# A linear-attention and SwiGLU kernel on one core: one more unit by squares, two more k turned through DRAM, and another set of weight pieces with signs by ScalarE

## The chip, the core and the metric

The kernel runs on one NeuronCore of a Trainium2 chip. The metric is the device time of one execution in microseconds (us). TensorE (PE) multiplies matrices and transposes by multiplying with an identity, VectorE (DVE) and ScalarE (ACT) work elementwise, GpSimd (POOL) and SyncE (SP) mainly issue DMAs. Each engine takes its instructions in the order in which they stand in its own queue and waits for semaphores of the others. A difference of less than some 0.2% can't be told from no change here.

## The reference

For 4 batches, 8 heads, 768 positions and head size 48 the reference runs a gated recurrence. Its output, 3072 tokens of 384 features, goes through a SwiGLU block with 1536 hidden features.

```
f = 1.0 / (1.0 + np.exp(-f_logit))
for t in range(S):
    state = f[:, :, t, :, None] * state + np.einsum('bhd,bhe->bhde', k[:, :, t], v[:, :, t])
    y[:, :, t] = np.einsum('bhd,bhde->bhe', q[:, :, t], state)
x = y.transpose(0, 2, 1, 3).reshape(B * S, H * D)
out = (silu(x @ w_gate) * (x @ w_val)) @ w_out
```

q, k, v and f_logit are float32. The three weight matrices come as float64, 8 bytes an element, and the kernel turns them into float32 itself.

## The kernel before

**Units.** The sequence is cut into 6 chunks of 128 positions. A unit is one batch's chunk, numbered u = 4 c + b for chunk c and batch b: units 0 to 3 are the first chunk, 4 to 7 the second, 8 to 11 the third. `attention(u)` (L576) is a generator of 15 steps that the caller spreads over time. In order: Sigmoid of f; gate turned into head-by-time form; k turned; reverse scan of the gates (`tail`); kT; (turn of kT); forward scan; q turned; qT and the decayed state; scores `sc` on TensorE; mask A; outputs y; the state's product dS; the new state.

**Two ways to turn f, k and q.** Time runs along the partitions when they are loaded, and the products want the features there. A plain unit loads them as they are, and TensorE transposes them: `fTp` (L614), `kTp` and `qTp` (L657, L658), four 128x128 transposes each. A unit by squares (`by_squares`, L403) loads them with four neighbouring positions side by side (L446 to L455), so that VectorE can transpose blocks of 32x32 (L630, L641, L685). Before, units from 5 on go by squares.

**Two ways to turn the decayed k back.** dS needs kT with time on the partitions again. Either TensorE transposes it (`kt`, L704) and ScalarE copies it out (L717), or the unit is `turned` (L634): VectorE transposes 32x32 blocks into `beside`, in the room of the raw k (L668), four DMAs write them to DRAM (L671), and one more reads them back as `kt` (L709 or L715). Before, units 5, 6, 7 and 10 to 19 are turned. In the second chunk the queue for that is GpSimd's, later SyncE's.

**Weights.** 18 pieces (`weight_piece`, L459): two column blocks each of w_gate and w_val in turn (pieces 0 to 11), then w_out (12 to 17). A piece is fetched by SyncE into one of four buffers. `sizes` (L487) on ScalarE makes the low bits (`up`) and the absolute value (`top`); `join` (L498) on VectorE clamps `top`, shifts it and adds `up`. The signs come either from VectorE (L514, one more instruction there, and the shift also masks, L512) or, for the pieces in `SIGNED` (L532), from ScalarE (L494) ahead of `top`; the shift is then L508. Pieces 0 and 1 are handled in two halves.

**Order of the work.** First the four units of chunk 0 (L1270 to L1294), with the first loads on SyncE's and GpSimd's queues (`load_ahead`, L1261) and the first sizes and joins. Then `mlp_plain` (L830) runs the block's 24 gate and val products for chunk 0 and its 12 down steps. For the other chunks, `mlp_fifteen` (L1006) computes each product of 3x3 by 3x2 blocks with 15 multiplications instead of 18, and `down_seven` (L1128) those of 2x2 blocks with seven instead of eight; both need sums of weight blocks, made by VectorE (`weight_sums`, L966). Everything else is put between TensorE's steps by hand-written times: in `in_turn_of_time` (L1222) each TensorE step has a nominal length, and whatever has a time at or below the sum so far is written into the queues ahead of the next step. `EARLY` (L937) holds the times of units 4 to 7, `SIZES_AT`, `JOINS_AT`, `FETCHES_AT` (L934 to L936) those of the weight pieces, `SUMS_AT` those of the weight sums, `CHAINS` (L913) those of the later units. An entry is only a place in the order; on the chip an instruction runs when its queue and its inputs let it. The order is held fast on TensorE, VectorE, ScalarE and SyncE (L1308, L1347); GpSimd's is free in the first stage apart from the chained loads (L454).

Of the kernel before, what the change touches and what calls it, by code (L numbers as in the profile page):

```python
# [13 lines left out]
AF = mybir.ActivationFunctionType  # L14
# [276 lines left out]
def short_path(ctx, tc, ident, least, judge, q, k, v, f_logit, moe_w_gate, moe_w_val, moe_w_out, out):  # L291
# [9 lines left out]
    nc = tc.nc  # L301
    B, H, S, D = q.shape
    C = 128
    NCH = S // C
# [7 lines left out]
    N1 = C + 1  # L312
    NRAW = 2
    NROT = 2
    NV = 4
    SQUARES = 2
# [23 lines left out]
    raw = {nm: [both_raw[nm][:, i] for i in range(NRAW)] for nm in "qkf"}  # L340
# [23 lines left out]
    def pairs(t, off=0):  # L364
        return t[:, off:off + HP * N1].rearrange("p (a t) -> p a t", t=N1)
# [35 lines left out]
    rooms = {nm: t.rearrange("p n h w -> p (n h w)")[:, 0:Q + HP * RUN] for nm, t in both_raw.items()}  # L401

    def by_squares(u):  # L403
        return u >= SQUARES * B - 3

    def make_rooms(pool):
        for nm in "fkq":
# [25 lines left out]
    def load(u, what="fkqv"):  # L433
        b, c = units[u]
        rows = slice(c * C, (c + 1) * C)
        inputs = dict(f=f_logit, k=k, q=q, v=v)
        for nm in "fqkv" if c >= SQUARES else "fvkq" if by_squares(u) else "fkqv":
            src = inputs[nm]
            if nm not in what:
                continue  # L440
            if nm == "v":
                dst = v_of(u)
            elif not by_squares(u):
                dst = raw[nm][u % NRAW]
            else:
                since = len(traced)  # L446
                for n in range(4):
                    at = Q * (1 - n % 2)
                    (nc.sync if c >= SQUARES else nc.gpsimd).dma_start(
                        out=rooms[nm][Q * n:Q * (n + 1), at:at + HP * RUN].rearrange("t (a e) -> t a e", a=HP),  # L450
                        in_=src[b, n // 2::2, rows, :].rearrange("a (t i) d -> t a (i d)", i=NI))
                if c < SQUARES:
                    by_pool.extend(ins for ins in traced[since:] if ins.engine == mybir.EngineType.Pool)
                    keep_order(by_pool[-5:])  # L454
                continue  # L455
            queue = nc.gpsimd if nm == "v" and c < SQUARES and (by_squares(u) or u in (1, 2)) else nc.sync
            queue.dma_start(out=dst[:, :, 0:D], in_=src[b, :, rows, :].rearrange("h t d -> t h d"))

    def weight_piece(dst, src, parts, signs):  # L459
# [69 lines left out]
    NW = 2  # L529
    FIRST = 2  # L530
    NPART = 2
    SIGNED = (4, 6, 7, 8, 9, 11, 15, 16, 17)  # L532

    def add_piece(dst, src, parts=1):
        fetch, *rest = weight_piece(dst, src, parts, len(fetches) in SIGNED)
        fetches.append(fetch)
        for group, fs in zip((sizes, joins), rest):
            group += fs
# [19 lines left out]

    def bank(name):
        return banks[-1].tile([128, 512], FP32, tag="a", name=name)  # L560

    ahead = set()

    def sigmoid_ahead(u):


        fr = raw["f"][u % NRAW]
        nc.scalar.activation(fr, fr, AF.Sigmoid)
        ahead.add(u)

    owner = {}

# [3 lines left out]
    def attention(u):  # L576
        b, c = units[u]
        rot = u % NROT if c < SQUARES else 0
        fr, kr, qr = (raw[nm][u % NRAW] for nm in "fkq")
        v_ = v_of(u)  # L580
        gate, tail = (x[u % NROT if c < SQUARES else 0] for x in (gates, tails))
# [3 lines left out]
        in_squares = by_squares(u)  # L585
# [32 lines left out]
        if in_squares:  # L618
            nc.scalar.activation(squares("f"), squares("f"), AF.Sigmoid)
            if c >= SQUARES and b == (c > SQUARES):  # L620

                nc.scalar.activation(spare, spare, AF.Silu)
        else:
            p = transposed("fTp", fr)
            for part in parts:
                nc.scalar.activation(pairs(gate)[:, part, 1:N1], p[:, part], AF.Copy if u in ahead else AF.Sigmoid)
        yield
        owner["gate", rot] = u
        if in_squares:
# [1 line left out]
            load_after(u, "f")  # L631
        yield

        turned = SQUARES * B + 2 <= u < (NCH - 1) * B or c < SQUARES and in_squares  # L634
        turn_queue = nc.sync if c >= SQUARES else nc.gpsimd
        kT = att.tile([128, HP, C], FP32, tag="kT", name="kT")
        qT = att.tile([128, HP, C], FP32, tag="qT", name="qT", bufs=2)
# [63 lines left out]
        if c < NCH - 1 and not turned:  # L701
            p = bank("kt")
# [27 lines left out]
        if c and b < B - 1:  # L730
# [20 lines left out]
            for h in range(H):  # L751
                a, par = h // 2, h % 2
                f = h * D
# [30 lines left out]
        if c < NCH - 1:  # L784
            p = bank("dS")
# [117 lines left out]
    def chain(k, q, qmul, turn=None, head=None):  # L903
        return (*[k + t for t in STEPS], turn or k + 3.5, head or k + 3.5, q, qmul)
# [6 lines left out]
        ((PRODUCT - 0.05, "b"), (between[1], "o"), (between[3], "o"), (down[3], "A")),  # L911
        *[((down[10] - whole, "A"), (between[1], "o"), (between[3], "o"), (down[3], "A"))] * (NCH - 4)))}
    CHAINS = {c: chains for c, chains in zip(range(2, NCH), (  # L913
        (chain(2.6, 4, 8.6), chain(14.5, 20, 23), chain(30, 37, 43.2), chain(57.4, 57.8, 61)),
        (chain(-12, -8.5, -5), chain(3.5, 6, 9), chain(16, 28, 33, 21.5, 23.5), chain(40.1, 53, 55, 44.5, 52)),
        *[(chain(-19.4, -11.2, -9.5), (-7.5, -6.3, 1.3, 2.2, 3.2, 5.5, 8, 10), chain(16, 28, 33, 21.5, 23.5), chain(40.1, 53, 55, 44.5, 52))] * (NCH - 4)))}
    LAST = 72.5
# [9 lines left out]
    def score_bank(u):  # L927
# [3 lines left out]
            return bank("sc")  # L931
        return {"o": banks_o, "A": banks_a}[kind].tile([128, 512], FP32, tag=kind, name="sc")

    JOINS_AT = (0.8, 4.5, 5, 7.6, 13.2, 16.3, 20.3, 27.2, 29.6, 36.1, 38.7, 43.3, 46.6, 47.8, 55.3, 55.4, 67.6, 70.8)  # L934
    SIZES_AT = (0.39, 2.4, 6.2, 11.1, 13.2, 18.4, 18.6, 22.1, 31.8, 38, 39.8, 40.1, 43.1, 50.8, 53, 56, 64.8)
    FETCHES_AT = (-1.1, 0.6, 5.5, 5.9, 6, 9.2, 10.6, 21.1, 23.6, 27, 35.5, 35.5, 37.8, 42.4)  # L936
    EARLY = (  # L937
        (-1.01, 4.17, 4.58, 9.7, 9.87, 10.5, 11, 11.5, 12, 13.4, 17.3, 22, 28.4, 28.41, 33),
        (26, 31.3, 32.8, 34.3, 34.6, 34.6, 36.1, 37.4, 38.2, 40.6, 43.3, 43.4, 50.8, 54.81, 56),
        (46.2, 49.2, 50.7, 51.4, 51.5, 57, 57.6, 58, 62, 63.9, 64.4, 65.5, 68.2, 68.21, 70),  # L940
        (63, 64, 66.8, 66.9, 67.4, 67.9, 68.6, 71.6, 73.3, 75.9, 76, 76.7, 78, 78.41, 80.3))
    SUMS_AT = (64.3, 64.5, 72.58, 72.7, 74.06, 74.74, 75.3, 75.42, 75.98, 76.02, 76.18, 76.3, 76.66, 76.86,
        77.34, 77.54, 78.22, 78.5, 79.18, 79.86, 81.22, 81.26, 81.26, 81.34, 81.62, 81.9, 81.94, 82.58, 82.58, 82.7,
        83.2)
    LATE_SUMS_AT = (23,)
    FINISH = (3, 5, 6, 7, 9, 10)
    DOWN_SUMS_AT = (5.2, 5.21, 18.8, 18.81, 34.5, 34.51, 43, 43.01)
    sums = {}

    def plus(dst, a, b):  # L950
# [310 lines left out]
    def load_ahead(u):  # L1261

        if u + NRAW < B:
            load(u + NRAW, "fkq")
        load(u + 1, "v")
        fetches.pop(0)()
        if u + NRAW == B:
            load(u + NRAW, "fkq")

    run(0, 0, 1, 2)  # L1270
    load_ahead(0)
# [11 lines left out]
            sizes.pop(0)()  # L1283
        run(b - 1, 4)
    first_join = joins.pop(0)
    first_join(("clamp"))
    sizes.pop(0)()
    run(B - 1, 3)
    first_join(("add"))
    joins.pop(0)()  # L1290
    next(first[B - 1])
    sizes.pop(0)()
# [2 lines left out]

    waiting = [(t, sizes.pop(0)) for t in SIZES_AT]
    waiting += [(t, joins.pop(0)) for t in JOINS_AT]
    waiting += [(t, fetches.pop(0)) for t in FETCHES_AT]
    assert not fetches and not sizes and not joins
    waiting.append((-0.02, lambda: sigmoid_ahead(B)))  # L1300
    for b, at in enumerate(EARLY):
        run_of = attention(B + b)
        waiting += [(t, lambda run_of=run_of: next(run_of)) for t in at]
# [1 line left out]
    sums = sums_of[0][0:7] + sums_of[1][0:7] + sums_of[0][7:] + sums_of[1][7:]  # L1305
    waiting += zip(SUMS_AT, sums[:len(SUMS_AT)])
    in_turn_of_time(waiting, mlp_plain(0))
# [17 lines left out]
    waiting = []  # L1325
# [4 lines left out]

    assert len(SUMS_AT) + len(LATE_SUMS_AT) == len(sums)
    waiting += zip(LATE_SUMS_AT, sums[len(SUMS_AT):])
    waiting += [(at, f) for at, f in zip(DOWN_SUMS_AT, down_weight_sums())]
    blocks = {}
# [90 lines left out]
```

## Time and profile before

| what | us |
|---|---|
| median of 3 runs | 597.67 (597.44 to 597.67) |
| the profiled execution | 597.51 |
| its span, first to last instruction | 595.8 |
| TensorE busy | 585.5 |
| VectorE busy | 479.3 |
| ScalarE busy | 301.1 |
| GpSimd busy | 112.8 |
| first gate product starts | 29.62 |
| first product of the fifteen starts | 138.44 |

The profiled execution's own time is its span and 1.7 us around it. The stages follow one another: the first chunk's units to 29.6 us, the plain block on chunk 0 with units 4 to 7 beside it to 138 us, then one round for each later chunk. Times in the trace count from the span's start. A timeline row gives start, length, engine, line of the kernel, operation, output<-input, shape and count, and in brackets the idle time of the engine just before it with what ended it. A row of a group gives busy time, mean ns of one instruction, and the idle time before. In the list of waits a row gives who waited for whom, the sum in us, how often, and the longest.

### The profile page before, as it was taken

What the parts mean: (1) busy time and instruction counts of PE and PEld (TensorE: products, weight loads), DVE (VectorE), ACT (ScalarE), POOL (GpSimd) and SP (SyncE); (2) the same over time, 40 slices, a digit from 0 to 9 for tenths busy, and PEclk for the clock granted to TensorE, in tenths of its full rate; (3) what the DMA queues carried; (4) which work ended last, traced back from release to release, by engine and by line L of the source; (5) the groups of instructions that cost most, each with busy time, mean ns of one, the idle gap of its engine ahead of it and who ended that gap; (6) DMA issues with size and microseconds to landing.
All of it is one profiled execution on the core that took longest, in us unless ns stands there. A gap on an engine that the chain in (4) does not pass through costs nothing.

```text
span 595.8 us, 10874 instructions
## 1 busy us (share of the span) xinstructions
PE 585.5 (98%) x3972; PEld 481.8 (81%) x3972; DVE 479.3 (80%) x830; ACT 301.1 (51%) x563; POOL 112.8 (19%) x240
## 2 busy tenths in 40 slices
PE   7899999999999999999999999999999999999996
PEld 4744444667888999888999888899988899988896
DVE  7997998999989877998986888994978972666741
ACT  3488677025877322676640667632476730356600
POOL 3140345202132330212030030330030330000000
PEclk9999999999999999999999999999999999999999
DMA  9999487233666565542345332543231100100001
GB/s 205 253 307 286 142 217 186 60 98 107 122 117 110 96 150 136 138 100 64 84 117 137 99 80 62 112 111 99 74 99 28 29 10 6 53 2 1 2 1 56
DMA packets 106291, 61.86 MB, mean 104 GB/s; under 512 B 64200, under 2 KB 97032, under 8 KB 106232
## 3 DMA queue, kind: packets, MB, share of 16 engines
q1 hardware_dynamic: 93800, 45.96, 31.0%
q0 software_dynamic: 10992, 13.19, 10.0%
q10 hardware_dynamic: 1440, 1.97, 0.9%
q8 instruction: 32, 0.52, 0.4%
q14 instruction: 27, 0.22, 0.1%
HBM read 47.64 MB, written 8.13 MB: 94 GB/s over the span
## 4 chain that ended last, share of the span: by engine, by line
PE 98%; DVE 1%; ACT 0%; issue 0%; DVEq 0%
PE o L1151 20%; PE A L1052 18%; PE B L1052 15%; PE c L1052 6%; PE o L1052 6%; PE o L859 5%; PE gate L836 5%; PE val L836 5%; PE sc L700 4%; PE o L1214 3%; PE y L746 3%; PE y L767 2%; PE dS L787 2%; PE y L742 2%; PE kt L704 1%; PE fTp L614 0%
## 5 line engine op out<-in xcount | busy, mean ns | idle before, releaser
L757 POOL DMA_DIRECT2D xT<-yT x120 | 59.8, 506 | 53.4 <-ACT yT L750 49.0
L1052 PE MATMUL A<-xs,w_both 128*128 128x256 f32 x240 | 62.2, 382 | 0.0
L1151 PE MATMUL o<-w_out,h 128*128 128x192 f32 x360 | 62.0, 327 | 0.0
L1151 PEld LDWEIGHTS o<-w_out,h 128*128 128x128 f32 x360 | 58.7, 190 | 1.0 <-issue 0.2
L1057 ACT COPY c<-A 128x512 f32<-128x512 f32 x40 | 23.3, 583 | 60.5 <-PE A L1052 59.4
L1057 ACT COPY aside<-A 128x512 f32<-128x512 f32 x60 | 35.2, 586 | 32.9 <-PE A L1052 32.7
L951 DVE TENSOR_TENSOR c<-c,aside 128x512 f32<-128x512 f32 x60 | 41.1, 685 | 12.8 <-ACT aside L1057 11.1
L1052 PEld LDWEIGHTS A<-xs,w_both 128*128 128x128 f32 x240 | 44.9, 190 | 6.6
L1004 DVE TENSOR_TENSOR h<-h,c 128x256 f32<-128x256 f32 x100 | 40.6, 414 | 7.6 <-ACT h L1068 7.3
L954 DVE TENSOR_TENSOR c<-c,aside 128x512 f32<-128x512 f32 x60 | 41.0, 684 | 2.7 <-ACT aside L1057 2.7
L1068 ACT ACTIVATE h<-c 128x256 f32<-128x256 f32 x100 | 39.4, 417 | 5.0 <-DVE c L951 3.8
L719 DVE TENSOR_TENSOR A<-sc,causal 128x512 f32<-128x512 f32 x48 | 30.9, 685 | 13.4 <-PE sc L700 13.4
L1151 PE MATMUL o<-ws,h 128*128 128x192 f32 x240 | 41.5, 328 | 0.0
L1052 PE MATMUL B<-xs,w_both 128*128 128x256 f32 x160 | 41.3, 380 | 0.0
L1052 PE MATMUL A<-xs,extra 128*128 128x256 f32 x160 | 41.2, 380 | 0.0
L1052 PE MATMUL c<-xT,w_both 128*128 128x256 f32 x160 | 41.1, 379 | 0.0
L1052 PE MATMUL B<-xT,extra 128*128 128x256 f32 x160 | 41.0, 379 | 0.0
L1057 ACT COPY aside<-B 128x512 f32<-128x512 f32 x60 | 35.2, 586 | 9.0 <-PE B L1052 7.0
L1151 PEld LDWEIGHTS o<-ws,h 128*128 128x128 f32 x240 | 39.1, 190 | 0.5
L954 DVE TENSOR_TENSOR c<-o,c 128x512 f32<-128x512 f32 x40 | 27.4, 686 | 11.0 <-ACT h L1068 6.2
L951 DVE TENSOR_TENSOR c<-c,o 128x384 f32<-128x384 f32 x15 | 8.2, 548 | 34.8 <-PE o L1151 34.8
L690 POOL MEMSET gates<- 128x4 f32 x24 | 3.6, 150 | 169.0 <-DVE qT L593 163.9
(163 smaller groups left out, 1240.2 us busy)
## 6 DMA issues: line engine op xcount, KB each, us to landing
fsquares<-in_f_logit_dram SPq DMA_DIRECT2D x64, 96.0 KB, 4.1
qsquares<-in_q_dram SPq DMA_DIRECT2D x64, 96.0 KB, 2.3
ksquares<-in_k_dram SPq DMA_DIRECT2D x64, 96.0 KB, 2.4
w<-in_moe_w_gate_dram SPq DMA_DIRECT2D x6, 768.0 KB
w<-in_moe_w_val_dram SPq DMA_DIRECT2D x6, 768.0 KB, 6.5
w<-in_moe_w_out_dram SPq DMA_DIRECT2D x6, 768.0 KB, 8.8
v<-in_v_dram SPq DMA_DIRECT2D x19, 192.0 KB, 2.8
turn<-ksquares SPq DMA_DIRECT2D x40, 64.0 KB, 2.2
```

The lines of the kernel that those rows point to most:

```text
L700: nc.tensor.matmul(sc[par][:, a * C:(a + 1) * C], lhsT=kT[r, a, :], rhs=qT[r, a, :], start=True, stop=True)
L719: nc.vector.tensor_tensor(A[:, par], sc[par].rearrange("p (a t) -> p a t", t=C), causal.unsqueeze(1).broadcast_to((128, HP, C)), ALU.mult)
L757: (nc.gpsimd if c >= SQUARES else nc.sync).dma_start(out=xT[c][f % 128:f % 128 + n, f // 128, b * C:(b + 1) * C], in_=yT[r:r + n, par, a / ...
L836: nc.tensor.matmul(p, lhsT=w[:, j, i, :], rhs=xT[c][:, i, :], start=(i == 0), stop=(i == KT - 1))
L859: nc.tensor.matmul(p, lhsT=hidden_tile(h, n // 2)[:, n % 2 * 2 + b // 2, b % 2 * C:(b % 2 + 1) * C], rhs=w_out[:, j, :], start=(n == 0), s ...
L951: nc.vector.tensor_tensor(dst, a, b, ALU.add)
L954: nc.vector.tensor_tensor(dst, a, b, ALU.subtract)
L1004: lagging.append(lambda: f(*args))
L1052: nc.tensor.matmul(p[name][:, n, :], lhsT=weights_of[a][:, n, j, :], rhs=tokens[b], start=fresh and n == 0, stop=True, skip_group_check=True)
L1057: nc.scalar.copy(t, p[name])
L1068: nc.scalar.activation(dst, src[:, 0, :], AF.Silu)
L1151: nc.tensor.matmul(p[:, n, :], lhsT=lhsTs[j][:, n * C:(n + 1) * C], rhs=rhs[:, j, :], start=first and j == order[0] and n == 0, stop=j == ...
```

## The change

- `by_squares` holds from unit 4 on, so unit 4's f, k and q are loaded in squares (from inside unit 3's step with kTp and qTp), its kT is turned through DRAM on GpSimd's queue, and its three sets of TensorE transposes and its kt go.
- Units 8 and 9 are turned through DRAM, too, on SyncE's queue.
- v of units 1 and 2 is loaded on SyncE's queue instead of GpSimd's, v of unit 4 on GpSimd's.
- `sigmoid_ahead`, a Sigmoid in place on the raw f of unit 4, is taken out.
- `SIGNED` names twelve pieces (0, 1, 2, 3, 5, 6, 9, 10, 11, 15, 16, 17) instead of nine (4, 6, 7, 8, 9, 11, 15, 16, 17).
- The tables of times change: weights, units 4 to 7, weight sums, and the chains of units 8, 9 and 10.

```diff
--- before.py
+++ after.py
@@ -401,7 +401,7 @@
     rooms = {nm: t.rearrange("p n h w -> p (n h w)")[:, 0:Q + HP * RUN] for nm, t in both_raw.items()}
 
     def by_squares(u):
-        return u >= SQUARES * B - 3
+        return u >= B
 
     def make_rooms(pool):
         for nm in "fkq":
@@ -453,7 +453,7 @@
                     by_pool.extend(ins for ins in traced[since:] if ins.engine == mybir.EngineType.Pool)
                     keep_order(by_pool[-5:])
                 continue
-            queue = nc.gpsimd if nm == "v" and c < SQUARES and (by_squares(u) or u in (1, 2)) else nc.sync
+            queue = nc.gpsimd if nm == "v" and c < SQUARES and by_squares(u) else nc.sync
             queue.dma_start(out=dst[:, :, 0:D], in_=src[b, :, rows, :].rearrange("h t d -> t h d"))
 
     def weight_piece(dst, src, parts, signs):
@@ -529,7 +529,7 @@
     NW = 2
     FIRST = 2
     NPART = 2
-    SIGNED = (4, 6, 7, 8, 9, 11, 15, 16, 17)
+    SIGNED = (0, 1, 2, 3, 5, 6, 9, 10, 11, 15, 16, 17)
 
     def add_piece(dst, src, parts=1):
         fetch, *rest = weight_piece(dst, src, parts, len(fetches) in SIGNED)
@@ -558,15 +558,6 @@
 
     def bank(name):
         return banks[-1].tile([128, 512], FP32, tag="a", name=name)
-
-    ahead = set()
-
-    def sigmoid_ahead(u):
-
-
-        fr = raw["f"][u % NRAW]
-        nc.scalar.activation(fr, fr, AF.Sigmoid)
-        ahead.add(u)
 
     owner = {}
 
@@ -623,7 +614,7 @@
         else:
             p = transposed("fTp", fr)
             for part in parts:
-                nc.scalar.activation(pairs(gate)[:, part, 1:N1], p[:, part], AF.Copy if u in ahead else AF.Sigmoid)
+                nc.scalar.activation(pairs(gate)[:, part, 1:N1], p[:, part], AF.Sigmoid)
         yield
         owner["gate", rot] = u
         if in_squares:
@@ -631,7 +622,7 @@
             load_after(u, "f")
         yield
 
-        turned = SQUARES * B + 2 <= u < (NCH - 1) * B or c < SQUARES and in_squares
+        turned = SQUARES * B <= u < (NCH - 1) * B or c < SQUARES and in_squares
         turn_queue = nc.sync if c >= SQUARES else nc.gpsimd
         kT = att.tile([128, HP, C], FP32, tag="kT", name="kT")
         qT = att.tile([128, HP, C], FP32, tag="qT", name="qT", bufs=2)
@@ -911,7 +902,7 @@
         ((PRODUCT - 0.05, "b"), (between[1], "o"), (between[3], "o"), (down[3], "A")),
         *[((down[10] - whole, "A"), (between[1], "o"), (between[3], "o"), (down[3], "A"))] * (NCH - 4)))}
     CHAINS = {c: chains for c, chains in zip(range(2, NCH), (
-        (chain(2.6, 4, 8.6), chain(14.5, 20, 23), chain(30, 37, 43.2), chain(57.4, 57.8, 61)),
+        (chain(2.6, 4.8, 8.6), chain(14.5, 21.7, 23.2, 21.2, 19.6), chain(29.2, 37, 43.6), chain(57.4, 55.8, 61)),
         (chain(-12, -8.5, -5), chain(3.5, 6, 9), chain(16, 28, 33, 21.5, 23.5), chain(40.1, 53, 55, 44.5, 52)),
         *[(chain(-19.4, -11.2, -9.5), (-7.5, -6.3, 1.3, 2.2, 3.2, 5.5, 8, 10), chain(16, 28, 33, 21.5, 23.5), chain(40.1, 53, 55, 44.5, 52))] * (NCH - 4)))}
     LAST = 72.5
@@ -931,20 +922,20 @@
             return bank("sc")
         return {"o": banks_o, "A": banks_a}[kind].tile([128, 512], FP32, tag=kind, name="sc")
 
-    JOINS_AT = (0.8, 4.5, 5, 7.6, 13.2, 16.3, 20.3, 27.2, 29.6, 36.1, 38.7, 43.3, 46.6, 47.8, 55.3, 55.4, 67.6, 70.8)
-    SIZES_AT = (0.39, 2.4, 6.2, 11.1, 13.2, 18.4, 18.6, 22.1, 31.8, 38, 39.8, 40.1, 43.1, 50.8, 53, 56, 64.8)
-    FETCHES_AT = (-1.1, 0.6, 5.5, 5.9, 6, 9.2, 10.6, 21.1, 23.6, 27, 35.5, 35.5, 37.8, 42.4)
+    JOINS_AT = (0.8, 2.1, 5, 7.6, 11.6, 15.9, 20.3, 25.6, 26, 34.9, 37.9, 42.9, 46.6, 48.2, 55.3, 55.4, 66.8, 70)
+    SIZES_AT = (0.39, 2.4, 6.2, 11.1, 13.2, 18.4, 18.6, 19.1, 30.2, 36.4, 38.2, 38.5, 43.1, 50.8, 54.2, 56, 66.8)
+    FETCHES_AT = (-1.1, 0.6, 5.9, 6.3, 7.2, 8.8, 10, 21.5, 23.6, 25.2, 29.3, 32.7, 40.8, 46.2)
     EARLY = (
-        (-1.01, 4.17, 4.58, 9.7, 9.87, 10.5, 11, 11.5, 12, 13.4, 17.3, 22, 28.4, 28.41, 33),
-        (26, 31.3, 32.8, 34.3, 34.6, 34.6, 36.1, 37.4, 38.2, 40.6, 43.3, 43.4, 50.8, 54.81, 56),
-        (46.2, 49.2, 50.7, 51.4, 51.5, 57, 57.6, 58, 62, 63.9, 64.4, 65.5, 68.2, 68.21, 70),
-        (63, 64, 66.8, 66.9, 67.4, 67.9, 68.6, 71.6, 73.3, 75.9, 76, 76.7, 78, 78.41, 80.3))
-    SUMS_AT = (64.3, 64.5, 72.58, 72.7, 74.06, 74.74, 75.3, 75.42, 75.98, 76.02, 76.18, 76.3, 76.66, 76.86,
-        77.34, 77.54, 78.22, 78.5, 79.18, 79.86, 81.22, 81.26, 81.26, 81.34, 81.62, 81.9, 81.94, 82.58, 82.58, 82.7,
-        83.2)
-    LATE_SUMS_AT = (23,)
+        (-0.02, 1, 3.6, 4.7, 6, 6.01, 7.2, 10.2, 10.2, 13.4, 17.3, 22, 29.6, 29.61, 35),
+        (26.4, 30.1, 31.6, 33.1, 34.2, 34.2, 35.7, 37.4, 37.8, 40.2, 44.1, 44.2, 51.6, 55.21, 58.2),
+        (46.2, 49.2, 51.5, 52.2, 52.3, 55, 55.2, 55.6, 59.6, 63.1, 63.6, 64.7, 67.4, 67.41, 69.2),
+        (62.2, 63.2, 66, 66.1, 66.6, 67, 67.1, 70, 72.5, 75.1, 75.6, 77.61, 78.3, 79.2, 80.3))
+    SUMS_AT = (63.5, 63.7, 71.78, 71.9, 73.26, 73.94, 74.5, 74.62, 75.18, 75.22, 75.38, 78.54, 78.74, 79.3,
+        79.42, 79.46, 79.46, 79.66, 79.7, 80.1, 80.38, 81.06, 82.02, 82.14, 82.42, 82.54, 82.78, 84.78, 85.26,
+        85.4, 86.5)
+    LATE_SUMS_AT = (22.25,)
     FINISH = (3, 5, 6, 7, 9, 10)
-    DOWN_SUMS_AT = (5.2, 5.21, 18.8, 18.81, 34.5, 34.51, 43, 43.01)
+    DOWN_SUMS_AT = (5.2, 5.21, 20.7, 20.71, 34.5, 34.51, 43, 43.01)
     sums = {}
 
     def plus(dst, a, b):
@@ -1262,10 +1253,9 @@
 
         if u + NRAW < B:
             load(u + NRAW, "fkq")
-        load(u + 1, "v")
+        if not by_squares(u + 1):
+            load(u + 1, "v")
         fetches.pop(0)()
-        if u + NRAW == B:
-            load(u + NRAW, "fkq")
 
     run(0, 0, 1, 2)
     load_ahead(0)
@@ -1283,10 +1273,10 @@
             sizes.pop(0)()
         run(b - 1, 4)
     first_join = joins.pop(0)
-    first_join(("clamp"))
+    first_join(("clamp",))
     sizes.pop(0)()
     run(B - 1, 3)
-    first_join(("add"))
+    first_join(("add",))
     joins.pop(0)()
     next(first[B - 1])
     sizes.pop(0)()
@@ -1297,7 +1287,6 @@
     waiting += [(t, joins.pop(0)) for t in JOINS_AT]
     waiting += [(t, fetches.pop(0)) for t in FETCHES_AT]
     assert not fetches and not sizes and not joins
-    waiting.append((-0.02, lambda: sigmoid_ahead(B)))
     for b, at in enumerate(EARLY):
         run_of = attention(B + b)
         waiting += [(t, lambda run_of=run_of: next(run_of)) for t in at]
```

## The prediction, made before the result was known

> **What bounds the kernel now.** I read the busy shares and the chain of waits first, then TensorE's waits, then each engine in order of time over 0 to 240 us.
>
> ```profile
> span 595.8 us, 10874 instructions
> PE 585.5 (98%) x3972; PEld 481.8 (81%) x3972; DVE 479.3 (80%) x830; ACT 301.1 (51%) x563; POOL 112.8 (19%) x240
> PE 98%; DVE 1%; ACT 0%; issue 0%; DVEq 0%
> PE idle L362 <- DVE floor L354: 2.1, 1, 2.1
> PE sc L700 <- DVE qT L593: 1.6, 2, 0.8
> PE fTp L614 <- DMA fraw<-in_f_logit_dram: 0.6, 1, 0.6
> ```
>
> The chain that ends last is 98% TensorE, and its few waits all lie before 29 us. The answer that adds busy time by stretch gives TensorE 30.00 of 30.00 us in each stretch from 30 us on, up to 500. So from the first gate product (29.62) to the last product (591) the time is the sum of what TensorE is given. An edit gains only if it takes instructions off TensorE, or, before 29.6 us, shortens the chain that leads there. It loses if an instruction that TensorE waits for comes after its place in TensorE's order. Busy time of a matmul overlaps that of the next, so I price TensorE work by the distance of starts:
>
> ```profile
> 39.92 0.60 PE L614 MATMUL kTp<-idf,kraw 128*128 128x128 f32 x4
> 40.36 0.60 PE L614 MATMUL qTp<-idf,qraw 128*128 128x128 f32 x4
> 40.80 5.32 PE L836 MATMUL gate<-xT,w_both 128*128 128x512 f32 x12
> 46.04 1.16 PE L700 MATMUL sc<-qT,kT 48*128 48x128 f32 x16
> 47.13 0.66 PE L704 MATMUL kt<-idf,kT 128*128 128x128 f32 x4
> 47.62 5.32 PE L836 MATMUL val<-xT,w_both 128*128 128x512 f32 x12
> ```
>
> Four transposes cost 0.44 us (39.92 to 40.36) or 0.49 us (47.13 to 47.62), though each is listed with 273 ns.
>
> **What the Trainium skill says.** "TensorE: Matmul & The Clock Gate", section Part 4: PE-mode transpose, puts one transpose at about 275 ns inside a kernel; the trace agrees on the duration (272 to 273 ns), but four in a row advance TensorE by only 440 to 490 ns, which is what I use. "VectorE: DVE Perf Modes", section The three transpose paths: VectorE transposes only within 32x32 blocks, hence the second half of the turn by DRAM; the trace shows it at 0.69 to 1.11 us for 128x512. "DMA: Bandwidth & Descriptors", section Issuing engines are not separate DMA queues: all queues end in the same 16 engines, so another queue saves issue time only. The trace agrees: the DMA share is 0.91 to 1.10 in every stretch from 15 to 60 us, whoever issues. "ScalarE: Activation LUTs", section Table sets, says that cheap functions lie in every set. The trace has a Sign at 66.12 between the Sigmoid of 60.04 and the next table load at 68.03, so signs ahead of the first Silu need no load.
>
> **The change, part by part.**
>
> 1. *Transposes off TensorE.* Unit 4 (first of the second chunk) loses fTp (29.13 to 29.62, 0.49), kTp and qTp (39.92 to 40.80, 0.88) and kt (47.13 to 47.62, 0.49). Units 8 and 9 lose kt (151.72 to 152.21 and 169.82 to 170.31, 0.49 each). Sum: 0.49 + 0.88 + 3 x 0.49 = **2.84 us**, all on the path.
>
> 2. *What fTp(4) covered.* It stood between dS(3) and the first gate product, which also needs ScalarE's copy of xT (28.67 to 29.15). dS(3) hands over at 29.12, so some 0.07 us of that copy comes into view.
>
> 3. *Signs.* The list goes from nine pieces to twelve: 0, 1, 2, 3, 5, 10 join it, 4, 7, 8 leave. Pieces 0 and 1 come in two halves.
>
> ```profile
> L494 ACT ACTIVATE up<-w,middle 128x768 f16<-128x768 uint16 x9 | 10.3, 1144 | 0.0
> L491 ACT ACTIVATE up<-w 128x384 uint16<-128x384 uint32 x4 | 2.6, 645 | 0.0
> L514 DVE TENSOR_SCALAR up<-w 128x768 uint16<-128x768 uint16 x7 | 4.2, 601 | 0.0
> L514 DVE TENSOR_SCALAR up<-w 128x384 uint16<-128x384 uint16 x4 | 2.3, 587 | 0.0
> L630 DVE STREAM_TRANSPOSE gates<-fraw 128x512 f32<-128x512 f32 x3 | 3.3, 1113 | 0.0
> L641 DVE STREAM_TRANSPOSE qT<-kraw 128x512 f32<-128x512 f32 x3 | 2.1, 684 | 0.0
> L685 DVE STREAM_TRANSPOSE tails<-qraw 128x512 f32<-128x512 f32 x3 | 2.1, 693 | 0.0
> L668 DVE STREAM_TRANSPOSE kraw<-kT 128x512 f32<-128x512 f32 x3 | 2.1, 706 | 0.0
> ```
>
> VectorE saves the sign step (0.62 between starts) but the shift then costs 0.59 instead of 0.47, so about 0.5 a piece or half: 4 halves + 4 - 3 = 5, or 2.5 us. ScalarE gains 4 half signs and one whole net. A half sign isn't in the trace; its ends are 0.50 (the half `up` start to start, 22.54 to 23.04) and 0.65 (that row's duration); I take 0.55. So 2.2 + 1.0 = +3.2 us; kt copies of units 4, 8, 9 (0.5 each) and the spare Sigmoid of L568 (0.5) leave, so -2.0.
>
> 4. *Unit 4 on VectorE.* Added: transposes of f 0.96, k 0.60, q 0.70, kT 0.63 and the small copy 0.07, by distance of starts in unit 5 (64.04 to 73.10): about +3.0 us. With part 3, +0.5 us up to 60 us, where VectorE idles 4.5 us at 56.2 to 60.8 for val. The stretch that matters is 28 to 45 us. I laid the new order out by hand from these distances. ScalarE: xT copied 29.05, third half 30.5, Sigmoid(4) 31.2, last half 32.8, piece 2 at 35.6, table load and first Silu 37.2, piece 3 at 40.0. VectorE: half joins and f's transpose to 34.1, k's transpose and scan to 36.0, piece 2 joined 38.1, kT 39.3, kT turned and second scan 41.2, piece 3 joined 43.2, q's transpose 43.9, **qT(4) done 44.6**. TensorE: gate from 29.15, four steps of 2.575, then 5.24 for two, so **sc(4) at 44.7**. Gates 2 and 3 want piece 2 at 39.45 (1.3 us to spare), the vals behind sc(4) want piece 3 at about 45.8 (2.6). sc(4) meets qT(4) almost to the tenth: I book 0.1 us, with ends 0 and 0.8.
>
> 5. *Loads.* f, k, q of unit 4 leave SyncE's queue (19.11 to 25.02) for GpSimd's, in runs of 768 instead of 192 bytes; v(4) goes there too; v(1) and v(2) go to SyncE's. f(4) may start once fTp(3) is through (18.2). The issue takes 2.2 us and the landing 7.3 more (page, fraw by POOL), so it should land near 28 to 30, before Sigmoid(4) wants it at 30.7: nothing booked. k(4) and q(4) follow kTp(3) and qTp(3) (22.7), wanted at 34 and 43. v(2), behind q(3) on SyncE (issued by 16.3), takes 4.0 to 7.0 to land; y(2) wants it at 22.77 and TensorE idles 0.79 after dS(2): nothing booked, ends -0.2 and +1.2. The weight fetches behind them wait on the same full engines as before.
>
> 6. *Before the gate.* Piece 0's sign step stood ahead of mask A(3) on VectorE (26.13 to 26.60), while sc(3) ended at 26.41: -0.1 us. Otherwise VectorE's own chain of about 5.13 us a unit sets this stage.
>
> 7. *Units 8 and 9.* VectorE +0.63 each for kT; TensorE gives 0.49 each. SyncE gets four turn DMAs and a kt load each (2.64 + 0.67), with k(9), k(10) and q behind them; units 10 to 19 already run so without a TensorE wait. qT(9) was done 166.5 for sc(9) at 168.73: 2.2 us less 2 x 0.63 less 0.49 leaves 0.5. VectorE is nearly full from 150 to 168, and TensorE's banks wait for ScalarE's copies, which wait for VectorE to free their buffers, so I book 0.2, ends 0 and 1.2.
>
> 8. *Retimed steps.* y(5) moves one step of TensorE's order later; weight sums move up to 3 us. The odd sums are wanted only at the third triple (138.4 + 26), so nothing is late: 0.
>
> Sum: -2.84 + 0.07 + 0.1 - 0.1 + 0.2 = **-2.57 us**. The profiled execution took 597.51 (span 595.8 and 1.7 around it): 594.94. The median, 597.67, is 0.16 above it: **595.1**.
>
> **Rivals.**
>
> *Partial give-back.* TensorE has less work but waits at sc(4), sc(9) or y(2). For: qT(4) has 0.1 us in hand and VectorE is over 90% busy in these stretches. Against: VectorE idles 4.5 us soon after. Price: the upper ends 0.8 + 1.2 with half of y(2)'s 1.2 give 2.6, less the 0.3 booked, half taken: +1.2, so 596.3.
>
> *f(4) behind others on GpSimd's queue, slower than before.* Sigmoid(4) stands on ScalarE ahead of the last half of val's first piece and of piece 2. If f(4) lands at L, qT(4) comes at 44.6 + (L - 30.7), and sc(4) holds TensorE as long. It eats the whole gain from L = 33.3. That happens if f(4) is issued behind the clearing of gates(3):
>
> ```profile
> 25.65 0.21 POOL L690 MEMSET gates<- 128x4 f32 x1
> 29.51 0.88 POOL L457 DMA_DIRECT2D v<-in_v_dram  x1 [3.65 <-PE dS L787]
> 31.61 2.23 POOL L449 DMA_DIRECT2D fraw<-in_f_logit_dram  x4 [1.22 <-ACT fraw L568]
> ```
>
> 25.9 + 2.2 + 7.3 = 35.4, so a stall of 4.7: 595.1 + 4.7 = 599.8. Against it: in this stage v(5) and v(6) are issued at 20.72 and 24.77, soon after what each waited for, not last.
>
> *The sum holds and more.* v(1), v(2) off GpSimd's early queue let f(1) land sooner (TensorE waited 0.6 us for it), no stall at all: 594.5.
>
> That the change doesn't do what it says touches only words: twelve pieces are signed in all, three more than before.
>
> **How the numbers follow.** Forecast as summed 0.60, within 594.6 to 595.9; partial give-back 0.22; slower 0.10; more 0.08. Some 0.2% (1.2 us) is what a measurement can tell from no change: faster means below 596.5. Give-back lies half below that and half above, mostly in "same": faster 0.60 + 0.08 + 0.10 = 0.78, same 0.12, slower 0.10. The range runs from 594.4 (all booked waits at their lower ends) to 597.4, the upper part of the give-back, leaving out the slower case and a few per cent below.
>
> **What would show it.** Right: 24 fewer TensorE transposes, gate from about 29.1, sc(4) without a wait, kt of units 4, 8, 9 by DMA. Wrong: ScalarE idle before Sigmoid(4) on a DMA, TensorE waiting at sc on qT near 44.7, or at y(2) on v; at units 8 and 9, waits of sc or of the products on ScalarE's copies.

## The result and the profile after

The changed kernel takes **602.41 us** (median of 7 runs, 599.87 to 604.09) against 597.67 before: a ratio of 1.0073, interval 1.0048 to 1.0097, so 0.73% slower. (Ratios here and below are estimated from all runs and lie near that of the means, not of the medians.) The forecast was 595.1 with a range of 594.4 to 597.4. The seven runs fall into two groups by the mean clock of TensorE in their records: 599.87 to 600.43 at 0.999 or 1.000, and 602.41 to 604.09 at 0.994 or 0.995. The profiled one, 603.93, is of the second group; before, it was 597.51.

The page of the changed kernel, span, busy shares, chain of waits and granted clock in 40 slices of 15 us:

```profile
span 602.2 us, 10869 instructions
PE 588.0 (98%) x3948; PEld 482.0 (80%) x3948; DVE 481.0 (80%) x832; ACT 302.0 (50%) x563; POOL 122.5 (20%) x256
PEclk9999799999999999999999999999999999999999
PE 85%; DMA 7%; DVE 4%; ACT 1%; issue 1%; POOL 1%; SPq 0%; DVEq 0%; ACTq 0%; POOLq 0%
```

TensorE has the 24 instructions less (3948 for 3972), and yet more busy time (588.0 for 585.5). The clock row, all 9 before, has a 7 in the slice from 60 to 75 us. The chain held 98% TensorE and no DMA; now 7% is DMA. TensorE's list of waits shows where it stands still (total, times, longest):

```profile
PE dS L778 <- DMA kt<-turn: 2.3, 1, 2.3
PE sc L691 <- DVE qT L584: 2.2, 3, 0.9
...
PE B L1043 <- ACT aside L1048: 0.8, 1, 0.8
...
PE c L1043 <- ACT c L1048: 0.4, 1, 0.4
```

In order of time on TensorE, with the idle time ahead of a row in brackets, first before and then after:

```profile
63.77 1.09 PE L746 MATMUL y<-A,v 128*64 128x128 f32 x16
64.69 0.62 PE L787 MATMUL dS<-v,kt 128*64 128x48 f32 x16
65.24 5.42 PE L836 MATMUL gate<-xT,w_both 128*128 128x512 f32 x12
70.50 5.31 PE L836 MATMUL val<-xT,w_both 128*128 128x512 f32 x12
```

```profile
45.26 1.16 PE L691 MATMUL sc<-qT,kT 48*128 48x128 f32 x16 [0.50 <-DVE qT L584]
...
62.60 1.09 PE L737 MATMUL y<-A,v 128*64 128x128 f32 x16
66.04 1.10 PE L778 MATMUL dS<-v,kt 128*64 128x48 f32 x16 [2.35 <-DMA kt<-turn]
67.07 7.96 PE L827 MATMUL gate<-xT,w_both 128*128 128x512 f32 x12
74.87 5.31 PE L827 MATMUL val<-xT,w_both 128*128 128x512 f32 x12
```

Up to y(4) the change works. The gate products start at 29.04 (29.62 before), sc(4) at 45.26 (46.04), the second part of y(4) at 62.60 (63.77): 1.17 us ahead. Then dS(4) waits 2.35 us for kT(4) from DRAM, and the dS takes 1.03 us to the next row instead of 0.55, and 12 gate products 7.80 instead of 5.26. The vals start at 74.87 instead of 70.50. In 12 us a lead of 1.17 has become a lag of 4.37. The view by stretch (the three columns at the end of a row are granted clock, DMA share of all engines, GB/s) shows the clock:

```profile
66.00:70.00 4.00, 3.96 (x20) 2.35 (x21) 3.90 (x8) 2.12 (x3) 2.71 (x4) 0.50 1.06 314
70.00:75.00 5.00, 5.00 (x10) 2.08 (x10) 2.07 (x4) 0.60 (x1) 0.22 (x1) 0.78 1.04 257
```

(The clock is 0.50 and 0.78; before it was 1.00 in both.) From there to the first product of the fifteen (142.82, before 138.44) the lag stays at 4.38. Units 8 and 9, which should bring 0.98 us, add 1.90: at 202.76, the first down product of the third chunk, the lag is 6.28.

Why kT(4) came late stands on GpSimd's queue:

```profile
40.82 2.88 POOL L662 DMA_DIRECT2D turn<-kraw  x4 [3.59 <-DVE kraw L659]
47.67 0.58 POOL L449 DMA_DIRECT2D kraw<-in_k_dram  x1 [3.97 <-DMA turn<-kraw]
...
50.61 2.18 POOL L449 DMA_DIRECT2D qraw<-in_q_dram  x4
52.83 0.71 POOL L706 DMA_DIRECT2D kt<-turn  x1
```

The loads of k(5) and q(5) are issued as the four turn DMAs land (from 47.67 on), the read of kt(4) only behind them, at 52.83, and it takes 13.08 us to land. From the first turn DMA to the landing of kt(4) it is 25.1 us.

At units 8 and 9 it is SyncE's queue: the four loads of k(9) overwrite the room from which unit 8's kT is being written to DRAM, so they stand behind that.

```profile
153.63 7.00 SPq L449 DMA_DIRECT2D ksquares<-in_k_dram  x4
```

```profile
162.55 0.71 DVE L632 STREAM_TRANSPOSE qT<-ksquares 128x512 f32<-128x512 f32 x1 [2.13 <-DMA ksquares<-in_k_dram]
```

```profile
167.77 1.13 PE L1043 MATMUL c<-xT,w_both 128*128 128x256 f32 x4 [0.41 <-ACT c L1048]
...
170.56 1.13 PE L1043 MATMUL B<-xT,extra 128*128 128x256 f32 x4 [0.80 <-ACT aside L1048]
```

VectorE, which waited for no DMA here before, waits 2.13 us for k(9). It frees the buffers of ScalarE's copies later (ScalarE waits 1.20 us for VectorE at 165.59), and these free TensorE's banks later.

### The profile page after: what moved, and what is told of

The parts are those of the page before. It is cut to its first block, busy times and chain, and to the rows that moved or that the text cites. A ratio compares the mean times of both kernels' runs of the same rounds, so it can differ in the third digit from the quotient of the medians.

```text
span 602.2 us, 10869 instructions
## 1 busy us (share of the span) xinstructions
PE 588.0 (98%) x3948; PEld 482.0 (80%) x3948; DVE 481.0 (80%) x832; ACT 302.0 (50%) x563; POOL 122.5 (20%) x256
## 4 chain that ended last, share of the span: by engine, by line
PE 85%; DMA 7%; DVE 4%; ACT 1%; issue 1%; POOL 1%; SPq 0%; DVEq 0%; ACTq 0%; POOLq 0%
PE o L1142 20%; PE A L1043 16%; PE B L1043 12%; PE o L850 5%; PE o L1043 5%; PE c L1043 5%; PE sc L691 4%; PE o L1205 3%; PE gate L827 3%; PE val L827 3%; DMA turn<-ksquares 2%; PE y L737 2%; DMA kt<-turn 2%; PE y L758 2%; PE dS L778 2%; PE y L733 1%
## 5 line engine op out<-in xcount | busy, mean ns | idle before, releaser
L827 PE MATMUL gate<-xT,w_both 128*128 128x512 f32 x72 | 35.2, 636 | 0.0
## 6 DMA issues: line engine op xcount, KB each, us to landing
w<-in_moe_w_val_dram SPq DMA_DIRECT2D x6, 768.0 KB, 12.3
```

What stands on the lines that cost most here:

```text
L827: nc.tensor.matmul(p, lhsT=w[:, j, i, :], rhs=xT[c][:, i, :], start=(i == 0), stop=(i == KT - 1))
```

## The experiments

The theory after this reading: (a) the round trip of kT(4) through DRAM delays dS(4); (b) the gap brings TensorE's clock down, which costs about as much again; (c) k(9) behind the turn of unit 8, not VectorE's own extra work, causes the waits at units 8 and 9. Rivals: the clock falls by itself or by the fuller DMA engines; VectorE's load gives the time back. All edits are against the changed kernel. Ratios are to the kernel before, run beside them (medians 597.54 to 597.61 us).

**1. kt(4) by TensorE.**

```diff
-turned = SQUARES * B <= u < (NCH - 1) * B or c < SQUARES and in_squares
+turned = SQUARES * B <= u < (NCH - 1) * B or c < SQUARES and u > B
```

> The changed kernel, but unit 4's kT is turned by TensorE (four transposes and ScalarE's copy) and not through DRAM. Theory: the changed kernel loses first at dS(4), where kt(4) lands 13.1 us after its issue and holds TensorE for 2.35 us, and TensorE's clock then falls for some 10 us and costs 3 us more in many of its runs. Both go and 0.49 comes back: about 598.0 against 597.67 of before, clock 1.000 in every run, no wait at dS(4), the waits of units 8 and 9 as they were. Rival 1, VectorE's added work is the cause: only 0.6 us of it goes, so the time stays at 600 or above and TensorE waits somewhere else in that stretch. Rival 2, the clock falls by itself and not after the wait: 0.994 stays in about half of the runs, and the time stays near 601.

598.0 us, ratio 1.0007 (0.9999 to 1.0015), with the clock at 0.998 or more in all 13 runs. No dS waits. The waits at units 8 and 9 stay (B 0.8, c 0.4 us). As (a) and (b) had it: 4.4 us go by giving TensorE 0.49 us of work back, to the number expected.

**2. kt of units 8 and 9 by TensorE.**

```diff
-turned = SQUARES * B <= u < ...
+turned = SQUARES * B + 2 <= u < ...
```

> The changed kernel, but units 8 and 9 keep TensorE's kt; unit 4 goes through DRAM. Theory: k(9) waits for the turn of unit 8 to leave the room of the raw k, comes 2.1 us late to VectorE, and TensorE's banks wait some 1.8 us and a slow stretch of 0.4 behind it. Without the turn these 2.2 us go and 0.98 comes back: 1.2 us less than the changed kernel, with dS(4)'s wait and the clock as they are there; 598.8 to 599.2 in runs at full clock, 601 to 602.5 in the others. Rival, VectorE's own load at units 8 and 9: the same sign, but VectorE's wait on the DMA of k would not be what goes. Second rival, the loss there is a late effect of the lower clock before: then the waits near sc(9) stay.

600.72 us, ratio 1.0038 (1.0020 to 1.0056): three runs at 597.8 to 598.08, four at 600.72 to 601.27. The profiled run, 598.08, has dS(4) waiting 1.32 us with the clock at 1.00 after it. From 138 to 200 us TensorE waits for nothing and VectorE for no DMA: in this stretch the lag on the kernel before grows by 0.13 us, where it grew by 1.90 in the changed kernel. So turning units 8 and 9 costs 1.8 us there, more than the 1.2 expected. The slower four runs are 3.0 us longer than the other three; no profile of one was kept, so whether the clock or a longer wait makes that is not shown by this run.

**3. kt(4) read back at once**, ahead of the loads of k(5) and q(5) on GpSimd's queue.

```diff
+            if u == B:
+                kt = att.tile([128, HP * C], FP32, tag="kt", name="kt")
+                turn_queue.dma_start(out=kt, in_=turn.rearrange("t i a r e -> i t (a r e)"))
+                by_pool.append(traced[-1])
             load_after(u, "k")
```

> The changed kernel, but kt(4) is read back on GpSimd's queue right after its turn, ahead of k(5) and q(5), which it stood behind. Theory: it is issued near 48 instead of 52.8; if the landing takes 8 to 13 us it is there at 56 to 61, before dS(4) wants it at 63.7, so the wait and the fall of the clock go with all of the transposes still off TensorE: about 597.5, clock 1.000. If the landing is so long only because the 16 engines are full of weight pieces and it lands when they are through, it lands at 65 to 66 all the same and the time stays near 602. VectorE-load rival: no change from the changed kernel.

598.46 us (598.05 to 601.9), ratio 1.0015 (1.0008 to 1.0021). kt(4) is issued at 48.98 and lands at 61.3, so dS(4) no longer waits, but the time missed the expectation by 1.0. GpSimd's queue shows a new wait:

```profile
48.98 0.70 POOL L666 DMA_DIRECT2D kt<-turn  x1 [2.04 <-DMA turn<-kraw]
49.67 2.21 POOL L449 DMA_DIRECT2D kraw<-in_k_dram  x4
51.87 1.63 POOL L449 DMA_DIRECT2D qraw<-in_q_dram  x3
61.57 0.55 POOL L449 DMA_DIRECT2D qraw<-in_q_dram  x1 [8.07 <-DMA kt<-turn]
```

The last quarter of q(5) is issued 8 us late. It is the eighth DMA behind kt(4), and in the trace's records the landings of GpSimd's DMAs are told by eight semaphores in turn: this issue waits for the one that kt(4) still holds. So it is the program's own semaphores that hold it. The read of kt(5), at 83.03, waits 2.80 us in the same way for the load of k(6) eight places ahead. In the profiled run (601.9, one of two among 23 above 599) dS(5) then waits 1.92 us for kt(5), followed by 12 val products in 6.95 us, with a clock of 0.66 from 95 to 100 us. In that run a wait came back one unit later; whether a smaller one there makes the 1.0 us of the median, no profile shows.

**4. As 3, with unit 8's kt by TensorE** (`SQUARES * B + 1 <= u`).

> As the run with kt(4) read back early, and unit 8 keeps TensorE's kt while unit 9 is turned. Theory: k(9) no longer stands behind a turn, so the waits before sc(9) go, 0.49 comes back: 597.5 - 2.2 + 0.5 = 595.8 to 596.2, faster than before by 0.25% to 0.3%. If VectorE's load at unit 9 is the cause, unit 9's 0.63 us still stands and some of the waits with it: 596.5 to 597.2.

596.60 us, ratio 0.9982 (0.9975 to 0.9990): 1.86 us below number 3, about the difference expected, with no wait of TensorE from 138 to 200 us. Like number 3 it stands above what was expected, by 0.4 us.

**5. As 3, with unit 8's kT turned in another buffer**, so that k(9) need not wait for it. Instructions of VectorE and the DMAs are the same as in 3.

```diff
+            own = u == SQUARES * B
+            if own:
+                kt = att.tile([128, HP * C], FP32, tag="kt", name="kt")
-            beside = rooms["k"][:, 0:HP * C]...
+            beside = (kt if own else rooms["k"][:, 0:HP * C])...
```

k(9) is loaded two steps earlier, right after its room has been transposed.

> kt(4) read back early, and both units 8 and 9 turned through DRAM as in the changed kernel, but unit 8's kT is turned in the buffer that kt(8) later fills instead of in the room of the raw k, so k(9) needn't wait for that turn. VectorE and the DMAs do the same work as in the changed kernel. Theory (k(9) stood behind the turn): the waits before sc(9) go with no transpose given back: 596.6 of the run with unit 8 by TensorE, less 0.49, so 596.0 to 596.2. Rival (VectorE's load at units 8 and 9): the waits stay, 598.0 to 598.5 as in the run with kt(4) early alone.

596.41 us, ratio 0.9981 (0.9973 to 0.9989). VectorE has the same work as in 3 and the waits B and c of units 8 and 9 are gone; only A waits 0.6 us later on, while VectorE still waits 2.0 us for k(10). This refutes the load of VectorE as the cause of those waits and shows (c).

**6. A gap without a DMA.** Number 1, with ScalarE's copy of kt(4) put behind y(4) and made three times.

```diff
+        if u == B:
+            for _ in range(3):
+                nc.scalar.copy(kt, p)
```

> Unit 4's kT by TensorE as in the first run, no DMA in it, but ScalarE's copy of kt(4) is put behind the outputs y(4) and made three times, so that dS(4) holds TensorE for some 2.3 us as kt's landing did. If the gap brings the clock down, whatever makes it: part of the runs at 598.0 + 2.3 = 600.3 with clock 1.000, the others near 603 with 0.994 to 0.995. If the clock fell because of the DMAs or by chance: all runs near 600.3.

601.86 us, ratio 1.0063 (1.0049 to 1.0076), 3.9 us above number 1.

```profile
65.71 0.67 PE L781 MATMUL dS<-v,kt 128*64 128x48 f32 x16 [2.19 <-ACT kt L778]
66.31 7.11 PE L830 MATMUL gate<-xT,w_both 128*128 128x512 f32 x12
```

The gap is 2.19 us, the rest of the loss slower products (6.95 us for the 12 instead of 5.25); the clock is 0.61 from 66 to 70 us at a DMA share of 0.71. This shows (b): a gap brings the clock down without a DMA. One of the five runs kept a mean clock of 0.999 and took 600.10, 2.1 us above number 1: the length of the gap alone.

**7. As 4, with the nine signs of before.**

```diff
-SIGNED = (0, 1, 2, 3, 5, 6, 9, 10, 11, 15, 16, 17)
+SIGNED = (4, 6, 7, 8, 9, 11, 15, 16, 17)
```

> The fourth run (596.6) with the nine signed pieces of before instead of the twelve. VectorE gets 0.5 us for each of the eight halves and pieces that leave the list ahead of or near qT(4), of which some 1 us fits into its waits on ScalarE. Theory that the signs made the room for unit 4's transposes: sc(4) waits for qT(4) 1.5 to 2.5 us instead of 0.5, so 598 to 599, with a fall of the clock in some runs. Rival, the signs do nothing: 596.6.

597.72 us, ratio 1.0009 (1.0002 to 1.0015): 1.1 us above number 4. Fifteen runs lie at 597.48 to 598.18, six at 599.10 to 599.58 with a mean clock of 0.996 or 0.997. In the profile, one of the faster:

```profile
46.76 1.16 PE L695 MATMUL sc<-qT,kT 48*128 48x128 f32 x16 [1.86 <-DVE qT L584]
```

sc(4) waits 1.86 us instead of 0.50. The signs by ScalarE are what lets VectorE have qT(4) in time: this part of the change pays, if a little less than was expected.

**8. As 5, with the join of piece 3 behind qT(4)** on VectorE (fourth entry of `JOINS_AT` 7.6 -> 10.25).

> As the run with its own room for unit 8, and VectorE joins weight piece 3 after qT(4) instead of before it. Theory: sc(4) waited 0.5 us for qT(4), which now is done 2 us sooner, while the vals behind sc(4), which had 2.6 us to spare for piece 3, still have about half a microsecond: 595.5 to 595.7. Rival: the vals now wait for piece 3, and the time is that of the run with its own room or up to 0.5 above.

596.08 us (595.66 to 597.37), ratio 0.9977 (0.9968 to 0.9987), above the 595.5 to 595.7 expected. sc(4) starts at 44.70 without a wait. Its interval overlaps that of number 5, so the step of 0.33 us is not settled. In the profiled run, at 597.15 one of the slowest of the ten, dS(5) waits 1.2 us for kt(5).

**9. As 8, with kt(4) by TensorE.**

> Unit 4's kt goes back to TensorE (0.49 us), units 8 and 9 stay turned through DRAM with unit 8's kT turned in the kt buffer and the later join of piece 3. No DRAM round trip stands before dS(4). Theory: the round trip of kT(4) costs elsewhere (k(5), q(5) later on GpSimd's queue) as much as its transposes bring. Then 598.0 (kt(4) by TensorE alone) less about 1.9 for the waits at units 8 and 9 gives 596.1, about the same as with kT(4) read early (596.1), and the runs scatter less. Rival, the round trip hides once the read is early: this kernel loses the whole 0.49 and comes to 596.5 or 596.6.

596.18 us (595.98 to 596.93), ratio 0.9974 (0.9963 to 0.9985). So turning kT(4) through DRAM brings nothing that could be measured even when it is read early. The profile of number 8 gives the 0.49 us off TensorE back by the 1.2 us that dS(5) waits; whether its faster runs do, no profile shows. In the profile of this one TensorE waits for no DMA from 26 to 140 us. What is left is one wait of VectorE in the third chunk, as in number 8:

```profile
173.71 0.71 DVE L632 STREAM_TRANSPOSE qT<-ksquares 128x512 f32<-128x512 f32 x1 [1.97 <-DMA ksquares<-in_k_dram]
```

That is k(10) behind the turn of unit 9. TensorE's lead on before is 2.23 us after sc(9) and 1.30 at 195 us.

**10. As 8, with later weight fetches**, to empty the DMA engines around kt(4).

```diff
-FETCHES_AT = (-1.1, 0.6, 5.9, 6.3, 7.2, 8.8, 10, 21.5, 23.6, 25.2, 29.3, 32.7, 40.8, 46.2)
+FETCHES_AT = (-1.1, 0.6, 5.9, 6.3, 7.2, 26, 28, 30, 32, 34, 36, 38, 40.8, 46.2)
```

> As the kernel with kT(4) read early, room for unit 8 and the later join, with the weight fetches of pieces 9 and 10 and those behind them 15 to 20 us later in SyncE's order, so that only piece 8's fetch shares the DMA engines with kt(4), k(5) and q(5). Theory, full engines make the landing long: kt(4) lands in 6 to 8 us instead of 10.5 to 12, the last q(5) load waits under 4 us for it, no dS waits for kt, and the time is 595.4 to 595.9 unless a piece of weights comes late. Rival, the read's own short runs make it long: it lands in 10 us or more again, and the time stays at 596.1.

600.03 us, ratio 1.0034 (1.0022 to 1.0046). The edit missed its aim: an entry is a place in SyncE's order, and SyncE still came to the fetches of pieces 9 and 10 at 48.22 and 51.42, as soon as their buffers were free. Those behind them fell in after the ten DMAs of xT (62.99 to 70.11), and the weights came late:

```profile
PE gate L835 <- ACT h L1003: 2.4, 1, 2.4
...
PE o L858 <- ACT h L1003: 1.2, 1, 1.2
```

From 50 to 60 us the DMA share was unchanged (1.07 and 1.04), and kt(4) took 10.4 us. What makes that landing long is not settled by this run.

**11. As 9, with unit 9's kt by TensorE too** (`and u != SQUARES * B + 1`).

> Unit 4's kt by TensorE, unit 8 turned in the kt buffer, unit 9's kt back on TensorE too. In the kernel that also turned unit 9, VectorE waited 2.0 us for k(10), which stood behind unit 9's turn on SyncE's queue, and TensorE was 2.23 us ahead of before at the products after sc(9) and only 1.30 us ahead at 195 us: 0.9 us given back. Theory, the queue: without unit 9's turn k(10) is early, 0.49 us of transposes come back, no wait is left, and the time is 597.6 - 1.8 = 595.8. Rival, VectorE's load in the stretch gives it back: one transpose less (0.7 us) of VectorE does not undo a loss of 0.9, and the time is 596.2 to 596.5.

596.06 us (595.94 to 596.36), ratio 0.9976 (0.9967 to 0.9985). No wait on k(10) is left, and from 31 to 300 us TensorE's list of waits is empty. The median lies between the queue's 595.8 and the 596.2 to 596.5 of VectorE's load; the profile decides for the queue. The lead after sc(9), 1.82 us, is kept whole at 195 us, and the last group of products starts 1.84 us ahead of before (585.10 for 586.94). The two profiled executions differ by 1.21 us (597.51 and 596.30): the other 0.63 goes in the last stores, which end 5.05 us after the last VectorE instruction here and 4.4 before.

**12. No kt of units 4, 8 and 9 through DRAM**; what is left is unit 4 by squares, the signs and the times.

> No kt of units 4, 8 and 9 goes through DRAM: only unit 4's squares (f, k, q by VectorE), the signs, the times of the changed kernel and the later join of piece 3. The traces put the first product of the fifteen starts 1.33 us ahead of before in that case, and nothing after that is taken off. Theory: 597.6 - 1.3 = 596.3, with no wait of TensorE on a DMA. If the time is 595.8 or less, turning units 8 and 9 never brought anything; if it is over 596.8, something in the retimed steps costs that I have not seen.

596.39 us (596.30 to 596.67), ratio 0.9981 (0.9974 to 0.9988), as expected. Against number 11, unit 8's turn is worth 0.33 us by the medians, whose intervals overlap, and 0.57 by the start of the last products in the profiles, when nothing waits for it; 0.49 was its price.

Numbers 8, 9 and 11 are the fastest, 1.4 to 1.5 us below the kernel before, and can't be told apart. Number 11 scatters least of the three.

## Why the prediction was wrong

**Part 1, transposes.** The sum was right where TensorE didn't wait. Number 12 has only fTp, kTp and qTp of it, 1.37 us: the fifteen start 1.34 us earlier, and the median falls by 1.15. Number 11 adds unit 8's kt. But "0.49 + 0.88 + 3 x 0.49, all on the path" counted each kt as taken off, when it was replaced by a round trip with an end of its own.

In the profiled execution, 9.0 us above the 594.94 of the sum, 5.5 lie at dS(4) and the products behind it and 2.7 at units 8 and 9 (1.90 lost where 0.78 was to be gained).

**The step that failed** is the missing term for kT(4) in parts 4 to 6. The prediction says of ScalarE that the "kt copies of units 4, 8, 9 (0.5 each)" leave, books f(4), k(4), q(4), v(4) as loads, and nowhere asks when kt(4) is back. The trace of before had the answer. Unit 5's round trip there, on GpSimd's queue:

```profile
68.90 2.92 POOL L671 DMA_DIRECT2D turn<-kraw  x4 [1.10 <-DVE kraw L668]
75.71 2.21 POOL L449 DMA_DIRECT2D kraw<-in_k_dram  x4 [3.88 <-DMA turn<-kraw]
77.91 2.19 POOL L449 DMA_DIRECT2D qraw<-in_q_dram  x4
80.14 0.71 POOL L715 DMA_DIRECT2D kt<-turn  x1
```

That kt lands 12.3 us later, at 92.4: 23.5 us from the first turn DMA, and dS(5) came at 94.3, so nothing waited. The prediction's own layout has kT(4) at 39.3; with 0.7 us for its turn and 0.3 to the first DMA, kt(4) comes at 63.8. dS(4), at 64.69 before, was to come 1.8 us earlier (0.49 + 0.88 + 0.49 less 0.07), at 62.9: a wait of 0.9 us could be read off. Measured were 25.1 us for the trip and 2.35 for the wait.

**The price of a gap.** The prediction priced each wait at its own length. Number 6 shows that a gap of 2.19 us costs 3.9 against number 1, and the changed kernel's three runs at the higher mean clock, 600.2 on average, lie 3.1 us below the four others (603.3). "TensorE: Matmul & The Clock Gate" of the Trainium skill, Part 1: The HAM clock gate (the "warmup" mystery), halves the clock after an idle window of about 3.4 us, and calls that window free-running. The traces agree on the half and on the window. The recorded clock is 1.00 or 0.50, and in each of the 14 profiles its changes lie whole multiples of 3.41 us apart: 58.03 us at full clock and then 6.83 at half in the changed kernel, 88.75 and 3.41 in number 3, 61.44 and 3.41 in number 6. Cut at these times, the stretches with the gaps are:

| profile | stretch of 3.41 us | TensorE busy in it, us | clock in the next one |
|---|---|---|---|
| changed kernel, dS(4) | 61.99 to 65.40 | 1.70 | 0.50 |
| number 3, dS(5) | 92.71 to 96.12 | 1.49 | 0.50 |
| number 6, dS(4) | 63.43 to 66.85 | 1.23 | 0.50 |
| number 10, gate | 83.35 to 86.76 | 2.17 | 1.00 |
| number 10, the same gap | 86.76 to 90.17 | 2.21 | 1.00 |
| number 7, sc(4) | 42.62 to 46.03 | 2.28 | 1.00 |
| number 8, dS(5) | 92.18 to 95.60 | 2.22 | 1.00 |
| number 2, dS(4) | 61.24 to 64.65 | 2.45 | 1.00 |

So the traces differ from the page in one thing: no whole window has to be idle. In all 14 profiles the clock fell after every stretch with TensorE busy for 1.70 us or less, and after none with 1.78 or more (number 11, 587.38 to 590.79); half of 3.41 is 1.71. Number 10's gap, 2.43 us and the longest of these, is cut in two by a boundary, and the clock stays. Each window at half clock costs up to half its length: 1.70 us for the 12 products in number 6. Where a gap falls against the windows would explain why only some runs of one kernel are slow; of no kernel were both a slow and a fast run profiled, so that is argued.

**Part 7, units 8 and 9.** Booked 0.2, ends 0 and 1.2. The queue was named ("with k(9), k(10) and q behind them") and then waved through with "units 10 to 19 already run so without a TensorE wait". The rooms are the same, the slack isn't: VectorE waits 2.13 us for k(9) and again for k(10). Numbers 1 and 12 differ by these two turns and by the later join, and sc(4) waits in neither; by medians number 1 is 1.6 us slower. So turning the two units cost some 1.6 us where a gain of 0.78 was counted.

**Parts 2 to 4** held. The gate products started at 29.04 (29.15 said), sc(4) waited 0.50 us (0.1 booked, ends 0 and 0.8), and moving one join takes that away (number 8). The half sign took 0.72 us, 0.58 from start to start, for the 0.55 taken. **Part 5** held for f(4) and v(2): neither is waited for. **Part 6** held (dS(3) starts 0.15 us earlier, 0.1 booked), and so did **part 8**: number 12, with all retimed steps, comes out as summed.

**The rivals.** The slower one named the right queue and the wrong transfer: f(4), which was in time, instead of kt(4), which stood at the end of it. The skill's "DMA: Bandwidth & Descriptors", section Issuing engines are not separate DMA queues, was cited for the engines all sharing; the runs agree (13.1 us for kt(4) at a share of 1.07, 7.2 in number 7, where it was 0.72 from 50 to 55 us), but that the share is the cause is argued from this pair, not shown.

**Open.** What makes kt(4)'s landing 7.2 us in one kernel and 10.4 to 13.1 in others; where the 1.0 and 0.4 us by which numbers 3 and 4 missed were lost.

## What to carry to other kernels

When work of the bounding engine is replaced by a round trip, add the trip up to its consumer's place, issue by issue on the queue that carries it, from the nearest trip in the trace; and look what the buffer that it leaves from holds up. Price a wait of a densely busy TensorE at more than its length: if it can leave TensorE idle for half of one of the 3.41 us stretches above, add what the next one loses at half clock. A stall saved may come back one unit later (numbers 3 and 8): read the next unit before booking it.

## What the runs showed of the hardware

- TensorE's granted clock changes at whole multiples of 3.41 us. It fell to 0.50 after stretches with 0.23 to 1.70 us of TensorE work, for 3.41 us (numbers 3 and 6) or 6.83 (changed kernel, where dS(4) still waited 0.64 us into them), and not after stretches with 1.78 us or more, though one gap was 2.43 us long (number 10). 12 products of 128x512 took 7.80, 6.95 and 6.95 us across a fall instead of some 5.2. The ends of matmuls are modelled in the profile, so the bound is rough.
- In all 14 profiles GpSimd's DMAs take eight semaphores in turn, so an issue can stand 8.07 us behind the landing of the eighth DMA before it (number 3: the fourth load of q(5) behind kt(4)).
- The read of a kt, 256 KB from DRAM, landed in 5.4 us at best and 13.1 at worst within one execution of the changed kernel.
